# A decode step of attention and a gated feed-forward: another second maximum, another way to turn q, another order of loads and of the first V products

## The chip, the cores and the metric

The kernel runs on one core of one Trainium2 chip. The metric is the device time of one execution in microseconds (us), as the median of several runs. All inputs lie in the chip's HBM at the start, and the output lies there at the end. Beside the timed runs one execution was taken with the hardware profiler; times inside the kernel come from that one.

The engines are named as in the profile: PE (matrix multiply; PEld is its weight load), DVE (vector), ACT (scalar, with the exp table), POOL (GpSimd) and SP (which issues the loads). Each works through its own list of instructions in order, and waits on semaphores for the others.

## The reference

Two batch rows `x` of 448 values are layer-normalised. Branch A is attention of one new token against the last 2048 cached positions (16 query heads, 8 key/value heads, head width 256). Branch B is a small ReLU network. The output is `x + A * silu(B)`.

```python
xn = layernorm(x)                                    # [2, 1, 448] bf16
q  = (xn @ wq).reshape(2, 1, 16, 256)                # wq [448, 4096]
k, v = k_cache[:, :, -2048:, :], v_cache[:, :, -2048:, :]   # 8 heads, each used by 2 query heads
p  = softmax(q . k * 256 ** -0.5)
s  = (p . v).reshape(2, 1, 4096) @ wo                # wo [4096, 448]
g  = silu(relu(xn @ w1) @ w2)                        # w1 [448, 1792], w2 [1792, 448]
out = x + s * g
```

## The kernel before, in words

**Units.** The 16 pairs of batch and key/value head are worked in four units (`NU`) of four heads of one batch row: unit u is head group u // 2 of batch row u % 2. The K and the V of a unit are 4 MB each; a partition holds 64 consecutive positions (`NT`) of one head, 256 values each. Three buffers `ub` take the eight loads in turn (`place`): k0, k1 and v0 first, then each load waits for the work that frees its buffer.

**The order of work** is written out by hand at the end of the function (lines 395 to 457). Each helper appends instructions to the engines' lists, with the operations each depends on; `_Prog.run` turns them into semaphore waits. So the order of the calls is the order on every engine.

- `do_turn(u)` (line 254): four DVE transposes turn K into `kt`, 32x32 blocks of 4-byte pairs. It frees k's buffer and needs the scores of the unit before, which read `kt`.
- `do_q()` (line 263): 28 matmuls over seven slots of `wq` put q into PSUM (`obk`), in four groups of partitions. Then ACT and DVE scale and spread the even and the odd values into `q_n` (128x1024 each), 16 matmuls turn them into `mbk`, and four ACT copies of 32 partitions each put them into `qz`, the weights of the score matmuls for all units.
- `do_S(u)` (line 291): 4 mask and 32 score matmuls into `sbk`.
- `do_chain(u)` (line 305): the softmax. DVE takes each partition's maximum (`rm`), PE turns that into one row, DVE takes the second maximum over the partitions of the same head (`mrow`, one partition, written 128 wide), PE spreads it over the partitions again, DVE copies it to `bias`, ACT takes exp, DVE and PE turn the result, and ACT copies it to `pt`.
- `do_sum(u)`, `do_PV(u)`, `do_o(u)` (lines 330, 335, 345): the sums of exp over each head and their reciprocals, 32 V matmuls into `obk`, the scaling into `o_sb`, and four matmuls and a product that put the unit's result into `at_exp`.
- `do_H()`, `do_F()` (lines 362, 380): branch B, two layers; then `wo` (lines 446 to 454), 128 matmuls into `wbk`, and the last two products.

The product with `wo` and the second layer of branch B run as four matmuls side by side, one for each quarter of the 448 columns, with two weight columns (the two batch rows); results lie on partitions 32 i + b.

**Queues.** SP issues all large loads, in the order of the `load` and `pr.dma` calls: k0, wq, k1, v0, k2 (after the turning of k0), v1 (after the turning of k1), k3 (after the V products of unit 0), v2, w1, v3, w2, and wo in five parts. An issue that waits holds up those behind it. ACT issues the loads of `x` and one of the two stores.

The line of the second maximum, of which the change speaks:

```python
v = pr.op(DVE, lambda e: e.tensor_reduce(
    out=view(mrow, 0, [[8, 16], [1, 8]], n=1), in_=view(mbk, 0, [[0, 16], [1, 8], [8, 16]], n=1),
    axis=AX.X, op=ALU.max, negate=True), [m])
```

It reads the 128 partition maxima sixteen times (the step 0 of the input), so that each of the 128 places gets the maximum of its own head.

Of the kernel before, what the change touches and what calls it, by code (L numbers as in the profile page):

```python
# [5 lines left out]
BF = mybir.dt.bfloat16  # L6
F32 = mybir.dt.float32
# [67 lines left out]
def bass_recurrent_scan__sliding_block_cached__dense_activation_relu__decode_kernel(  # L75
# [22 lines left out]
    NU = 4  # L98
# [9 lines left out]
    with es:  # L108
# [27 lines left out]
        xr = named("xr", [128, SLOTS * 4], BF)  # L136
        q_n = named("q_n", [128, 2048], BF)
        qz = named("qz", [128, NU * 8 * 32], BF)
        fold8 = named("fold8", [128, 8], F32)
        h_n = named("h_n", [128, FC], BF)  # L140
        h_sb = named("h_sb", [128, 28], BF)
        x_c = named("x_c", [128, NCOL], BF)
# [13 lines left out]
        at_exp = named("at_exp", [128, 256], BF)  # L156
        at2 = named("at2", [128, 64], BF)
        wqo = named("wqo", [128, 32 * D], BF)
# [16 lines left out]
        def kv_src(u, cache):  # L175
# [5 lines left out]
        p_xc = pr.op(POOL, lambda e: e.memset(x_c[:, :], 0.0))  # L181
        d_xc = [pr.dma(ACTE, view(x_c, 0, [[1, NCOL]], n=4, p0=b, pstep=32),
                       A_x[b, 0, :].rearrange("(i n) -> i n", i=4), [p_xc]) for b in range(B)]

# [13 lines left out]
        p_one = pr.op(POOL, lambda e: e.memset(one_f[:, :], 1.0), [p_idf])  # L198
        p_qz = pr.op(POOL, lambda e: e.memset(qz[:, :], 0.0))

# [19 lines left out]
        def fold_op(e):  # L220
            with nc.allow_low_precision("zeros and ones"):
                return e.tensor_reduce(out=fold[:, :], in_=view(ident, 0, [[1, 32], [32, 4]]), axis=AX.X, op=ALU.add)
        v_fold = pr.op(DVE, fold_op)
        v_fold8 = pr.op(DVE, lambda e: e.tensor_reduce(
            out=fold8[:, :], in_=view(ident, 0, [[1, 8], [8, 16]]), axis=AX.X, op=ALU.add), [p_id])
# [27 lines left out]

        def do_turn(u):
            src = ub[place[f"k{u}"]]
            s32, k32 = src[:, :].bitcast(F32), kt[:, :].bitcast(F32)
            for g in range(4):
                lo, hi = g * UW // 8, (g + 1) * UW // 8
                st["turn", u, g] = pr.op(DVE, lambda e, lo=lo, hi=hi: e.transpose(k32[:, lo:hi], s32[:, lo:hi]),  # L259
                                         [dma_of[f"k{u}"], st.get(("S", u - 1))])  # L260
            freed[f"k{u}"] = st["turn", u, 3]

        def do_q():
            deps = [d_wq, v_xr, st["obz"]]
            for s in range(SLOTS):
                for i in range(4):
                    lo = s * HC + i * 512
                    o = pr.op(PE, mm(obk[32 * i:32 * i + 4, :], xr[:, 4 * s:4 * s + 4], wqo[:, lo:lo + 512],
                                     s == 0, s == SLOTS - 1, tile_position=(0, 32 * i)), deps)
                    deps = []  # L270
            st["q_mm"] = o
            a_z0 = st["obz"]
            v = pr.op(ACTE, lambda e: e.activation(  # L273
                view(q_n, 0, [[256, 8], [32, 4], [1, 32]]), view(obk, 0, [[64, 8], [0, 4], [2, 32]]),
                ACT.Copy, scale=SCALE), [o, a_z0])
            v2 = pr.op(DVE, lambda e: e.tensor_scalar(  # L276
                out=view(q_n, 128, [[256, 8], [32, 4], [1, 32]]), in0=view(obk, 1, [[64, 8], [0, 4], [2, 32]]),
                scalar1=SCALE, scalar2=None, op0=ALU.mult), [v])
            deps = [v, v2, st["mbk"]]
            for ch in range(2):  # L280
                for wp in range(8):
                    o = pr.op(PE, mm(view(mbk, 32 * wp + ch, [[2, 16]]),
                                     view(q_n, 128 * (8 * ch + wp), [[1, 128]]),
                                     view(ident, 0, [[2, 2], [1, 2], [32, 4]]), True, True), deps)
                    deps = []
            for Q in range(4):
                st["q"] = st["mbk"] = pr.op(ACTE, lambda e, Q=Q: e.activation(  # L287
                    view(qz, 8 * Q, [[256, NU], [32, 8], [1, 8]], n=32, p0=32 * Q),
                    view(mbk, 0, [[8, NU], [32, 8], [1, 8]], n=32, p0=32 * Q), ACT.Copy), [o, p_qz])

        def do_S(u):
            deps = [st["q"], st.get(("exp", u - 1)), v_am] + [st["turn", u, g] for g in range(4)]
            for wp in range(-1, 8):
                for g in range(4):
                    if wp < 0:
                        lhsT, rhs = amask[:, :], view(ident, 0, [[0, 128], [1, 4]])
                    else:
                        lhsT = view(qz, 256 * u + 32 * wp, [[1, 32]])
                        rhs = view(kt, g * UW // 4 + 64 * (wp // 2) + wp % 2, [[256, 16], [2, 32]])
                    o = pr.op(PE, mm(sbk[32 * g:32 * g + 32, :], lhsT, rhs, wp < 0, wp == 7,  # L300
                                     tile_position=(0, 32 * g)), deps)
                    deps = []
            st["S", u] = o

        def do_chain(u):
            v = pr.op(DVE, lambda e: e.tensor_reduce(out=rm[:, :], in_=sbk[:, :], axis=AX.X, op=ALU.max),  # L306
# [3 lines left out]
            v = pr.op(DVE, lambda e: e.tensor_reduce(  # L310
                out=view(mrow, 0, [[8, 16], [1, 8]], n=1), in_=view(mbk, 0, [[0, 16], [1, 8], [8, 16]], n=1),
                axis=AX.X, op=ALU.max, negate=True), [m])
            m = pr.op(PE, mm(mbk_ap(128, 1), mrow[0:1, :], one_f[0:1, :], True, True), [v, p_one])
            v = st["mbk"] = pr.op(DVE, lambda e: e.tensor_copy(bias[:, :], mbk_ap(128, 1)), [m])  # L314
            a = st["exp", u] = pr.op(ACTE, lambda e: e.activation(  # L315
                e_sb[:, :], sbk[:, :], ACT.Exp, bias=bias[:, 0:1], accum_out=ssum[:, 0:1]),
                [v, st.get(("ptd", u - 1)), st.get(("gs", u - 1))])
            t = st["ptd", u] = pr.op(DVE, lambda e: e.transpose(ptd[:, :], e_sb[:, :]), [a, st.get(("sp", u - 1))])  # L318
            deps = [t, st.get(("pt", u - 1))]
# [15 lines left out]
        def do_PV(u):  # L335
            v, p = ub[place[f"v{u}"]], pt[u % 2]
            deps = [dma_of[f"v{u}"], st["pt", u], st.get(("osb", u - 1)), st["q"]]
            for k in range(NT // 2):
                g = k % 4
                o = pr.op(PE, mm(obk[32 * g:32 * g + 16, :], view(p, 16 * k, [[1, 16]]),  # L340
                                 v[:, 512 * k:512 * k + 512], k < 4, k >= 28, tile_position=(0, 32 * g)), deps)
                deps = []
            st["PV", u] = freed[f"v{u}"] = o
# [18 lines left out]
        def do_H():  # L362
# [11 lines left out]
            for j in range(7):  # L374
                o = pr.op(PE, mm(fbk[:, 4 * j:4 * j + 4], view(h_n, j, [[7, 128]], n=4), ident[0:4, 0:4], j == 0), deps)
                deps = []
            st["hT"] = pr.op(DVE, lambda e: e.tensor_copy(
                view(h_sb, 0, [[2, 7], [14, 2], [1, 2]]), view(fbk, 0, [[4, 7], [2, 2], [1, 2]])), [o])

        def do_F():  # L380
            deps = [st["w2"], st["hT"], st["fbz"]]
            for f in range(14):
                for i in range(4):
                    lo = f * D + i * NCOL
                    o = pr.op(PE, mm(fbk[32 * i:32 * i + B, 0:NCOL], h_sb[:, 2 * f:2 * f + 2], w2_sb[:, lo:lo + NCOL],
                                     f == 0, f == 13, tile_position=(0, 32 * i)), deps)
                    deps = []
# [5 lines left out]
                out=g_sb[:, :], in0=fbk[:, 0:NCOL], in1=tmp[:, :], op=ALU.mult), [v_rc])  # L393

        load("k0")
        d_wq = pr.dma(SP, wqo[:, 0:SLOTS * HC], wq_src)
        load("k1")
# [4 lines left out]
        do_turn(0)  # L402
        load("k2")
        do_q()
        do_S(0)
        do_chain(0)
        do_sum(0)
        do_turn(1)
        load("v1")
        do_PV(0)  # L410
        load("k3")
        do_o(0)
        do_S(1)
        do_chain(1)
# [25 lines left out]
        for b in range(2):  # L440
            m_at = pr.op(PE, mm(mbk_ap(256 + 32 * b, 32), at_exp[:, 128 * b:128 * b + 128],
                                fold[:, :], True, True), [st["at", 3], v_fold, st["mbk"]])
            v_at2 = st["mbk"] = pr.op(DVE, lambda e, b=b: e.tensor_copy(
                view(at2, b, [[2, 32]]), mbk_ap(256 + 32 * b, 32)), [m_at])
        do_F()
        deps = [v_at2, st["wbz"]]
        landed = dict(d_wo)
        for j in range(32):
            deps = deps + [landed.get(j)]
            for i in range(4):  # L450
                lo = j * D + i * NCOL
                m_o = pr.op(PE, mm(wbk[32 * i:32 * i + B, 0:NCOL], at2[:, 2 * j:2 * j + 2], wqo[:, lo:lo + NCOL],
                                   j == 0, j == 31, tile_position=(0, 32 * i)), deps)
                deps = []
        v_t = pr.op(DVE, lambda e: e.tensor_tensor(
            out=tmp[:, :], in0=wbk[:, 0:NCOL], in1=g_sb[:, :], op=ALU.mult), [m_o, st["g"]])
        v_o = pr.op(DVE, lambda e: e.tensor_tensor(
            out=out_sb[:, :], in0=tmp[:, :], in1=x_c[:, :], op=ALU.add), [v_t, *d_xc])
        d_o = [pr.dma((SP, ACTE)[b], out[b, 0, :].rearrange("(i n) -> i n", i=4),
                      view(out_sb, 0, [[1, NCOL]], n=4, p0=b, pstep=32), [v_o]) for b in range(B)]  # L460
        pr.op(ACTE, None, d_o)

# [29 lines left out]
```

## Time and profile before

| | us |
|---|---|
| median of 3 runs | 126.58 (125.11 to 126.99) |
| the profiled execution, its own time | 126.08 |
| its span, first to last instruction | 124.6 |
| DVE busy / PE busy / ACT busy | 63.6 / 48.0 / 12.5 |
| transposes of K (`kt`), 16 of 2.28 | 35.5 |
| score matmuls / V matmuls, 128 each | 14.0 / 11.6 |
| second maximum (`mrow`), 4 of 2.28 | 9.1 |
| PE waiting for `wq` | 15.9 |

The kernel moves 44.19 MB, on average 355 GB/s over the span. The span in 40 slices of 3.1 us, each digit the busy share in tenths:

```profile
PE   0100000924814380951300496140019516779561
DVE  2620799130172999145599514549980653110341
ACT  2700000038004000002100000210000021000000
PEclk9999999999995555578555559655556995555897
DMA  5797999989798998989899969989997999700000
```

PEclk is the clock granted to PE in tenths of full speed. The runs of 9 on DVE are the turnings of K, the last 15 us have no loads, and no compute engine is busy throughout.

Times after this are microseconds from the span's start, unless they are durations. The chain of waits is the work that ended last, followed back from the last instruction to what released it; it is read as the list of pieces that set the time.

### The profile page before, as it was taken

To read this page: it belongs to the slowest core of one execution; us is meant where nothing else is said; L and a number is where in the kernel's file an instruction comes from. 1 tells how busy PE (TensorE), PEld (TensorE's weight loads), DVE (VectorE), ACT (ScalarE), POOL (GpSimd) and SP (SyncE) were. 2 spreads that over 40 slices of the span, in tenths; PEclk is the share of its full clock that TensorE was granted. 3 is DMA by queue.
4 is the path that set the end of the run, shared out by engine and by line. 5 is a ranking of instruction groups with operands and counts; after the bars stand their busy time and mean duration, and the time that the engine had idled before them with its cause. 6 is when DMAs were issued, how large, how long until landed. Compare 5 with 4: busy or idle time off the path is not lost.

```text
span 124.6 us, 1421 instructions
## 1 busy us (share of the span) xinstructions
PE 48.0 (39%) x630; PEld 20.5 (16%) x630; DVE 63.6 (51%) x69; ACT 12.5 (10%) x24; POOL 2.3 (2%) x11
## 2 busy tenths in 40 slices
PE   0100000924814380951300496140019516779561
PEld 0000000211112110310200131130003204114150
DVE  2620799130172999145599514549980653110341
ACT  2700000038004000002100000210000021000000
POOL 6000000000000000000000000000000000000000
PEclk9999999999995555578555559655556995555897
DMA  5797999989798998989899969989997999700000
GB/s 169 337 505 337 442 442 463 484 358 505 337 505 373 463 473 368 326 358 494 347 494 410 410 263 426 463 345 510 389 484 329 425 418 421 300 6 0 0 5 1
DMA packets 2474, 44.19 MB, mean 355 GB/s; under 512 B 291, under 2 KB 549, under 8 KB 933
## 3 DMA queue, kind: packets, MB, share of 16 engines
q1 hardware_dynamic: 2440, 44.11, 84.2%
q8 instruction: 4, 0.07, 0.2%
q10 hardware_dynamic: 28, 0.00, 0.0%
q14 instruction: 2, 0.01, 0.0%
HBM read 44.11 MB, written 0.00 MB: 354 GB/s over the span
## 4 chain that ended last, share of the span: by engine, by line
DVE 37%; PE 36%; DMA 16%; ACT 5%; issue 4%; SPq 1%
DVE kt L259 20%; DMA wqo<-in_A_wq_dram 16%; PE sbk L233 13%; PE obk L233 9%; DVE mrow L310 7%; PE fbk L233 5%; PE mbk L233 5%; ACT e_sb L315 3%; DVE ptd L318 2%; DVE o_sb L347 2%; PE pbk L233 2%; PE wbk L233 1%; ACT qz L287 1%; DVE rm L306 1%; DVE h_n L370 1%
## 5 line engine op out<-in xcount | busy, mean ns | idle before, releaser
L259 DVE STREAM_TRANSPOSE kt<-ub 128x2048 f32<-128x2048 f32 x16 | 35.5, 2277 | 6.2 <-DMA ub<-in_A_k_cache_dram 6.2
L233 PE MATMUL sbk<-kt,qz 128*32 128x512 bf16 x128 | 14.0, 611 | 0.0
L233 PE MATMUL obk<-ub,pt 128*16 128x512 bf16 x128 | 11.6, 525 | 2.2 <-DMA ub<-in_A_v_cache_dram 2.2
L306 DVE TENSOR_REDUCE rm<-sbk 128x1 f32<-128x512 f32 x4 | 2.8, 692 | 18.0 <-PE sbk L233 18.0
L310 DVE TENSOR_REDUCE mrow<-mbk 1x128 f32<-1x2048 f32 x4 | 9.1, 2278 | 3.7 <-PE mbk L308 3.7
L233 PE MATMUL sbk<-ident,amask 128*32 128x512 bf16 x16 | 2.5, 608 | 19.8 <-DVE kt L259 18.2
L233 PE MATMUL obk<-wqo,xr 128*4 128x512 bf16 x28 | 3.2, 626 | 15.9 <-DMA wqo<-in_A_wq_dram 15.9
L315 ACT ACTIVATE e_sb<-sbk,bias 128x512 bf16<-128x512 f32 x4 | 2.7, 687 | 61.9 <-DVE bias L314 61.9
L233 PEld LDWEIGHTS sbk<-kt,qz 128*32 128x32 bf16 x128 | 4.7, 140 | 7.6 <-issue 7.6
L233 PE MATMUL fbk<-w_sb,xr 128*4 128x448 bf16 x14 | 5.5, 571 | 0.7 <-DVE h_n L370 0.7
L233 PE MATMUL mbk<-one_f,mrow 1*128 1x1 f32 x8 | 1.7, 281 | 9.5 <-DVE mrow L310 9.5
L233 PE MATMUL pbk<-ptd,ident 128*32 128x128 bf16 x64 | 2.5, 307 | 7.2 <-DVE ptd L318 7.2
L233 PEld LDWEIGHTS obk<-ub,pt 128*16 128x16 bf16 x128 | 3.9, 112 | 8.2 <-issue 4.7
L347 DVE TENSOR_SCALAR o_sb<-obk,rs 128x512 bf16<-128x512 f32 x4 | 2.9, 731 | 3.3 <-PE obk L233 3.3
L318 DVE STREAM_TRANSPOSE ptd<-e_sb 128x512 bf16<-128x512 bf16 x4 | 2.8, 711 | 3.4 <-ACT e_sb L315 3.4
L370 DVE TENSOR_SCALAR h_n<-fbk 4x448 bf16<-4x448 f32 x2 | 1.2, 612 | 5.3 <-PE fbk L233 5.3
L233 PEld LDWEIGHTS sbk<-ident,amask 128*32 128x32 bf16 x16 | 0.4, 101 | 20.1 <-DVE kt L259 18.3
L233 PEld LDWEIGHTS obk<-wqo,xr 128*4 128x4 bf16 x28 | 0.8, 114 | 17.5 <-DMA wqo<-in_A_wq_dram 16.0
L233 PE MATMUL mbk<-fold,o_sb 128*128 128x8 bf16 x16 | 1.1, 172 | 6.6 <-DVE o_sb L347 6.6
L276 DVE TENSOR_SCALAR q_n<-obk 128x1024 bf16<-128x1024 f32 x1 | 1.2, 1225 | 3.9 <-ACT q_n L273 3.9
L333 DVE RECIPROCAL rs<-mbk 128x1 f32<-128x1 f32 x4 | 0.7, 168 | 4.9 <-PE mbk L233 4.9
L233 PEld LDWEIGHTS mbk<-one_f,mrow 1*128 1x128 f32 x8 | 1.4, 213 | 10.2 <-DVE mrow L310 10.2
(63 smaller groups left out, 39.1 us busy)
## 6 DMA issues: line engine op xcount, KB each, us to landing
ub<-in_A_k_cache_dram SPq DMA_DIRECT2D x4, 4096.0 KB, 25.6
ub<-in_A_v_cache_dram SPq DMA_DIRECT2D x4, 4096.0 KB, 17.3
wqo<-in_A_wq_dram SPq DMA_DIRECT2D x1, 3584.0 KB, 20.3
w_sb<-in_B_w_dram SPq DMA_DIRECT2D x2, 1568.0 KB, 20.6
wqo<-in_A_wo_dram SPq DMA_DIRECT2D x2, 1120.0 KB, 27.3
wqo<-in_A_wo_dram SPq DMA_DIRECT2D x1, 896.0 KB, 30.1
wqo<-in_A_wo_dram SPq DMA_DIRECT2D x2, 224.0 KB, 30.2
x_c<-in_A_x_dram ACTq DMA_DIRECT2D x2, 0.9 KB
```

The costliest lines, as they stand in the source:

```text
L233: return lambda e: e.matmul(out_ap, lhsT=lhsT, rhs=rhs, start=start, stop=stop, skip_group_check=True, **kw)
L259: st["turn", u, g] = pr.op(DVE, lambda e, lo=lo, hi=hi: e.transpose(k32[:, lo:hi], s32[:, lo:hi]), [dma_of[f"k{u}"], st.get(("S", u - 1))])
L276: v2 = pr.op(DVE, lambda e: e.tensor_scalar(out=view(q_n, 128, [[256, 8], [32, 4], [1, 32]]), in0=view(obk, 1, [[64, 8], [0, 4], [2, 32]]) ...
L287: st["q"] = st["mbk"] = pr.op(ACTE, lambda e, Q=Q: e.activation(view(qz, 8 * Q, [[256, NU], [32, 8], [1, 8]], n=32, p0=32 * Q), view(mbk, ...
L306: v = pr.op(DVE, lambda e: e.tensor_reduce(out=rm[:, :], in_=sbk[:, :], axis=AX.X, op=ALU.max), [st["S", u]])
L310: v = pr.op(DVE, lambda e: e.tensor_reduce(out=view(mrow, 0, [[8, 16], [1, 8]], n=1), in_=view(mbk, 0, [[0, 16], [1, 8], [8, 16]], n=1), a ...
L315: a = st["exp", u] = pr.op(ACTE, lambda e: e.activation(e_sb[:, :], sbk[:, :], ACT.Exp, bias=bias[:, 0:1], accum_out=ssum[:, 0:1]), [v, st ...
L318: t = st["ptd", u] = pr.op(DVE, lambda e: e.transpose(ptd[:, :], e_sb[:, :]), [a, st.get(("sp", u - 1))])
L333: st["rs", u] = st["mbk"] = pr.op(DVE, lambda e: e.reciprocal(rs[:, u:u + 1], mbk_ap(130, 1)), [st["gs", u]])
L347: st["osb", u] = pr.op(DVE, lambda e: e.tensor_scalar(out=o_sb[:, :], in0=obk[:, :], scalar1=rs[:, u:u + 1], scalar2=None, op0=ALU.mult), ...
L370: st["h_n"] = pr.op(DVE, lambda e, u=u: e.tensor_scalar(out=h_n[0:4, u * (FC // 2):(u + 1) * (FC // 2)], in0=fbk[0:4, 0:FC // 2], scalar1= ...
```

## The change

It does six things.

- The second maximum is taken into a tile `m8` of 1x8, reading the 128 values once, and a copy then spreads it to the 128 places of `mrow`.
- q is turned in another way: one ACT copy of 128x512 out of PSUM, one DVE transpose in 32x32 blocks of 4-byte pairs, four matmuls against `rep4` (made at the start by four DVE products), and eight DVE products with `qmask` that write `qz`, two for each unit. Scores of a unit depend on that unit's two.
- The first slot of `wq` is a load of its own ahead of k0, the other six follow k0, and the q matmuls are split the same way.
- The first quarter of the turning of k1 is placed on DVE between the exp of unit 0 and the transpose of its result.
- The V products and the output step of unit 0 stand behind the scores of unit 1.
- Batch row 1 lies 16 partitions from row 0 in place of 1, in `x_c`, `out_sb` and the results of the last two layers; so `x_c` is loaded, and the output stored, in one DMA each, and the weights `h_sb` and `at2` are 17 columns wide, with zeros between the two.

```diff
-        d_xc = [pr.dma(ACTE, view(x_c, 0, [[1, NCOL]], n=4, p0=b, pstep=32),
-                       A_x[b, 0, :].rearrange("(i n) -> i n", i=4), [p_xc]) for b in range(B)]
+        d_xc = pr.dma(ACTE, view(x_c, 0, [[1, NCOL]], n=8, pstep=16),
+                      A_x[:, 0, :].rearrange("b (i n) -> i b n", i=4), [p_xc])
...
-        p_qz = pr.op(POOL, lambda e: e.memset(qz[:, :], 0.0))
+        p_at = pr.op(POOL, lambda e: e.memset(at2[:, :], 0.0))
+        p_h = pr.op(POOL, lambda e: e.memset(h_sb[:, :], 0.0))
...
+        for i in range(4):
+            v_r4 = pr.op(DVE, lambda e, i=i: e.tensor_scalar(
+                out=view(rep4, 128 * i, [[32, 4], [1, 32]]), in0=view(fold, 0, [[0, 4], [1, 32]]),
+                scalar1=qmask[:, i:i + 1], scalar2=None, op0=ALU.mult), [v_fold, v_qm])
...
+        def do_q():
+            a = pr.op(ACTE, lambda e: e.activation(q_n[:, :], obk[:, :], ACT.Copy, scale=SCALE),
+                      [st["q_mm"], st["obz"]])
+            st["q_n"] = a
+            v = pr.op(DVE, lambda e: e.transpose(q_t[:, :].bitcast(F32), q_n[:, :].bitcast(F32)), [a])
+            deps = [v, v_r4, st["mbk"]]
+            for i in range(4):
+                o = pr.op(PE, mm(mbk_ap(64 * i, 64), rep4[:, 128 * i:128 * i + 128],
+                                 view(q_t, 0, [[64, 8], [1, 8]]), True, True), deps)
+                deps = []
+            for u in range(NU):
+                for par in range(2):
+                    st["qz", u] = st["mbk"] = pr.op(DVE, lambda e, u=u, par=par: e.tensor_tensor(
+                        out=view(qz, 256 * u + 32 * par, [[64, 4], [8, 4], [1, 8]]),
+                        in0=view(mbk, 2 * u + par, [[8, 4], [0, 4], [32, 8]]),
+                        in1=view(qmask, 0, [[0, 4], [1, 4], [0, 8]]), op=ALU.mult), [o, v_qm])
...
             v = pr.op(DVE, lambda e: e.tensor_reduce(
-                out=view(mrow, 0, [[8, 16], [1, 8]], n=1), in_=view(mbk, 0, [[0, 16], [1, 8], [8, 16]], n=1),
-                axis=AX.X, op=ALU.max, negate=True), [m])
+                out=m8[:, :], in_=view(mbk, 0, [[1, 8], [8, 16]], n=1), axis=AX.X, op=ALU.max, negate=True), [m])
+            v = pr.op(DVE, lambda e: e.tensor_copy(
+                view(mrow, 0, [[8, 16], [1, 8]], n=1), view(m8, 0, [[0, 16], [1, 8]], n=1)), [v])
...
+            if between:
+                between()
             t = st["ptd", u] = pr.op(DVE, lambda e: e.transpose(ptd[:, :], e_sb[:, :]), [a, st.get(("sp", u - 1))])
...
-                    o = pr.op(PE, mm(fbk[32 * i:32 * i + B, 0:NCOL], h_sb[:, 2 * f:2 * f + 2], w2_sb[:, lo:lo + NCOL],
+                    o = pr.op(PE, mm(fbk[32 * i:32 * i + 17, 0:NCOL], h_sb[:, 32 * f:32 * f + 17], w2_sb[:, lo:lo + NCOL],
...
+        d_wq = [pr.dma(SP, wqo[:, 0:HC], wq_src[:, 0:HC])]
         load("k0")
-        d_wq = pr.dma(SP, wqo[:, 0:SLOTS * HC], wq_src)
+        d_wq.append(pr.dma(SP, wqo[:, HC:SLOTS * HC], wq_src[:, HC:SLOTS * HC]))
         load("k1")
         load("v0")
...
+        do_q_mm(0, 1)
+        do_q_mm(1, SLOTS)
         do_q()
         do_S(0)
-        do_chain(0)
+        do_chain(0, lambda: do_turn(1, 0, 1))
         do_sum(0)
-        do_turn(1)
+        do_turn(1, 1, 4)
         load("v1")
+        do_S(1)
         do_PV(0)
         load("k3")
         do_o(0)
-        do_S(1)
         do_chain(1)
...
-                m_o = pr.op(PE, mm(wbk[32 * i:32 * i + B, 0:NCOL], at2[:, 2 * j:2 * j + 2], wqo[:, lo:lo + NCOL],
+                m_o = pr.op(PE, mm(wbk[32 * i:32 * i + 17, 0:NCOL], at2[:, 32 * j:32 * j + 17], wqo[:, lo:lo + NCOL],
...
-        d_o = [pr.dma((SP, ACTE)[b], out[b, 0, :].rearrange("(i n) -> i n", i=4),
-                      view(out_sb, 0, [[1, NCOL]], n=4, p0=b, pstep=32), [v_o]) for b in range(B)]
-        pr.op(ACTE, None, d_o)
+        d_o = pr.dma(ACTE, out[:, 0, :].rearrange("b (i n) -> i b n", i=4),
+                     view(out_sb, 0, [[1, NCOL]], n=8, pstep=16), [v_o])
+        pr.op(ACTE, None, [d_o])
```

## The prediction

> **What bounds the kernel now.** I read the page's shares of the chain first, then that chain in order of time, then the timeline around each join, then the loads one by one. The page's chain shares and its line for the load queue:
> ```profile
> q1 hardware_dynamic: 2440, 44.11, 84.2%
> ...
> DVE 37%; PE 36%; DMA 16%; ACT 5%; issue 4%; SPq 1%
> ```
> The load queue is nearly always full until about 110 us, yet the chain goes through a load only once, at the start. After that DVE and PE hand the work to each other, and each saved microsecond on that hand-over counts as long as the loads stay ahead. The chain in order of time (start us, us, what):
> ```profile
> 1.46 20.29 DMA wqo<-in_A_wq_dram
> ...
> 21.78 3.19 PE obk L233 x28
> ...
> 24.99 1.03 ACT q_n L273
> ...
> 26.05 1.24 DVE q_n L276
> ...
> 27.42 0.65 PE mbk L233 x16
> ...
> 29.25 0.39 ACT qz L287
> ...
> 29.68 4.06 PE sbk L233 x36
> ...
> 34.81 2.29 DVE mrow L310
> ```
> From the end of the q matmuls (24.97) to the first scores (29.68) nothing but turning q happens: 4.71 us. Then comes the second maximum, 2.29 us, in every unit. The timeline where unit 0 meets unit 1:
> ```profile
> 40.59 4.49 DVE L259 STREAM_TRANSPOSE kt<-ub 128x2048 f32<-128x2048 f32 x2
> ...
> 42.64 2.74 PE L233 MATMUL obk<-ub,pt 128*16 128x512 bf16 x24 [2.17 <-DMA ub<-in_A_v_cache_dram]
> ...
> 49.39 0.71 DVE L347 TENSOR_SCALAR o_sb<-obk,rs 128x512 bf16<-128x512 f32 x1
> ...
> 50.75 3.63 PE L233 MATMUL sbk<-kt,qz 128*32 128x512 bf16 x32
> ...
> 54.44 0.69 DVE L306 TENSOR_REDUCE rm<-sbk 128x1 f32<-128x512 f32 x1 [3.75 <-PE sbk L233]
> ```
> The V products of unit 0 wait for v0 (42.6), but run beside the turning of k1, which sets the pace until 49.47. The issues of k1 (at 2.06) and v0 (at 2.79), with the time from issue to landing last:
> ```profile
> ub<-in_A_k_cache_dram SPq DMA_DIRECT2D x1, 4096.0 KB, 29.4
> ```
> ```profile
> ub<-in_A_v_cache_dram SPq DMA_DIRECT2D x1, 4096.0 KB, 39.8
> ```
> So k1 lands at 31.5 and v0 at 42.6. From the same view: k0 13.2, wq 21.8, k2 52.4, v1 62.1, k3 71.9, v2 84.0, w1 87.7, v3 97.5, w2 101.2, the last of wo about 110.
>
> **First wq slot, then k0.** The first slot is a seventh of 3.67 MB, 0.52 MB; at the 420 GB/s of those stretches k0 lands 1.3 us later, 14.5, and its turning (8.89 us) ends at 23.4 instead of 22.14. The scores will ask for it at 26.6, so 3.2 us of cover hide it; anything beyond counts in full. wq and k0 together are the same bytes, so wq's rest still lands at 21.8. Slot 0's 4 of 28 matmuls are done long before, and they stand in front of nothing but the other slots. The last 24 take 3.19 - 0.43 = 2.76 (four take 0.427 in the timeline). Ahead of them on DVE, four `rep4` products (0.17 to 0.23 each by L228 and L226) and on POOL two memsets (0.95 by L199, and under half of it) end before 8 us: hidden behind wq. k2's issue slips from 22.17 to 23.4, with k1 and v0 still queued ahead: nothing.
>
> **q turned on DVE.** After the matmuls: ACT copy of 128x512, 0.60 (L327); transpose of 128x256 f32, 0.35 (a 2048-wide one takes 2.277, so 0.28 and a start; upper end 0.71, L318); four matmuls, 0.33 (16 of the old ones took 0.64, four against `fold` 0.27); two products of 128x128, 0.58 (0.275 at 112 wide, L455); hand-overs 0.22. Sum 2.08 against 4.71. Scores of unit 0 start at 21.78 + 2.76 + 2.08 = 26.6, not 29.68: **-3.1** (-2.5 to -3.4). The other six products, 1.7 us of DVE, lie under the 4.06 us of scores, before `rm` needs DVE.
>
> **Second maximum.** A reduce of 128 elements to 8 costs 0.28 to 0.37 (L217, L224) and a 128-wide copy 0.23 (L226); with a hand-over 0.59 against 2.29. All four are on the chain with DVE waiting for nothing else: 4 x 1.70 = **-6.8** (-6.4 to -7.0).
>
> **A quarter of k1's turning during exp.** DVE idles from the end of `bias` to `ptd`, 0.84 us. The quarter (2.28) fills it and pushes `ptd` back, but the quarter has to be done anyway and DVE carries the chain here: **-0.8**. It adds a wait: `ptd`, and with it pt, the sum and the rest of the turning, now stand behind k1. `bias` ends at 37.73 - 3.1 - 1.7 = 32.9 and k1 lands at 31.5: 1.4 us in hand. Turning then ends at 49.47 - 3.1 - 1.7 - 0.8 = 43.9.
>
> **V products behind the scores.** PE now runs S1 and PV0 in one piece from 43.9, v0 long landed. On DVE `osb` and `at` of unit 0 still stand ahead of `rm` of unit 1, so S1's maximum waits for PV0 as well. Before, from the end of turning to `rm`: 54.44 - 49.47 = 4.97. After: S1 and PV0, then `osb` 0.72, four matmuls 0.27, `at` 0.24, hand-overs 0.15. How long S1 and PV0 take hangs on the granted clock; the windows that compare are units 2 and 3, with H before the last PV:
> ```profile
> core 0: us, PE busy (x) PEld busy (x) DVE busy (x) ACT busy (x) POOL busy (x), PEclk, DMA share, GB/s
> ...
> 49.47:54.44 4.97, 4.23 (x40) 1.39 (x40) 0.85 (x3) 0.00 (x0) 0.00 (x0) 0.50 0.87 316
> ...
> 70.14:76.51 6.37, 6.32 (x69) 2.21 (x69) 0.69 (x1) 0.00 (x0) 0.00 (x0) 0.60 0.87 327
> ...
> 92.86:98.18 5.32, 5.27 (x69) 2.15 (x69) 0.69 (x1) 0.00 (x0) 0.00 (x0) 0.73 0.94 397
> ...
> 105.25:112.67 7.42, 6.01 (x26) 1.90 (x29) 1.45 (x3) 0.00 (x0) 0.00 (x0) 0.50 0.42 166
> ```
> The same pair took 6.3 in unit 2 and 5.3 in unit 3; at half clock throughout it is 4.06 + 3.6 = 7.65. I take 6.0: 7.4 against 4.97, **+2.4** (+1.7 to +4.1). The Trainium skill, "TensorE: Matmul & The Clock Gate", Part 1, says that about 3.4 us of sustained work in a free-running window lifts the clock. By it the pair would take an estimated 5.5 to 7.2 us and the kernel 117.4 to 119.1, but the last window above held 0.50 through 7.4 us at 81% busy, so the rule is no promise.
> PV0 ends at 49.9, so k3 is issued as before (50.07); v1, ahead of it on SP, goes from 49.49 to 43.9, v2 and v3 go about 5 us earlier. k3 (by 71.9) is needed at 77, v2 (by 84) at 90, v3 (by 97.5) at 104, wo's first rows (earlier than 110, as the dips of the load rate near 50 and 71 us close) at 111. The loads stay hidden; the closest is wo.
>
> **Seventeen weight columns, one store, one load of x_c.** 184 matmuls in F and W load 17 columns instead of 2. The W loads start 12.3 ns apart (101 in 1.31 us, mean 84 ns); the 32-column loads of `pbk` start 14.7 ns apart (16 in 0.35, mean 129). Between 0 and 184 x 2.4 ns = 0.44: I take **+0.2**. The same page of the Trainium skill, section "LDWEIGHTS (loading the stationary operand)", charges columns/1.2 ns, an estimated 12.5 ns more each, 2.3 us in all and 120.0 in the end if every load stood in line; the `pbk` loads start closer together than that rule's own time for one. The store takes about 2.0 us from `out_sb` to the end either way, 0 (-0.1 to +0.2): the two issues ran side by side (0.66 and 0.56). The 1.14 us in which PE waits inside W for no data stay, as far as I can tell (0 to -1.1). One x_c load fewer saves 0.56 of ACT's issue at 1.3 us, beside nothing.
>
> **Sum.** -3.1 - 6.8 - 0.8 + 2.4 + 0.2 = -8.1. The profiled execution has a span of 124.6 in a time of 126.08, so 1.48 around it: 116.5 + 1.5 = 118.0. The median shown, 126.58, lies 0.5 above that execution, inside the spread of 125.1 to 127.0; I predict **118.0**.
>
> **Rivals.**
> - *PE prices at their upper end*: S1 and PV0 at half clock (+1.7) and the weight loads in line (+0.4, or past it by up to 1): 120 to 121. For it, S1 ran at 0.50 and H held 0.50 throughout; against it, both pairs of this length lifted the clock. 0.14.
> - *PE speeds up early*: with the q step shorter, the q matmuls and S0 follow within 2.1 us and the clock lifts inside S0. It gains up to 1.4, until `bias` meets k1's landing, and with unit 1's pair at 5.3: 115.9. Against it, S0 ran at the slow pace 4.7 us behind the same matmuls. 0.08.
> - *The wait for k1 takes the place of what was saved* (slower). If the engines serve k1 and v0 side by side, k1 lands with v0 at 42.6, the quarter starts 9.7 us after `bias` and all of unit 0 behind it slips by that: 118.0 + 9.7 = 127.7. It decides from a landing at 41.0 (32.9 + 8.1); past 44 the kernel is slower by over 2%. For it, three loads are queued at once and v0's issue stands 0.7 behind k1's. Against it, landings come in order of issue (13.2, 21.8, 31.5, 42.6), 8.6 to 11.1 apart as their bytes at 380 to 430 GB/s would have it. 0.04.
> - *The change doesn't do what it says*: the small reduce stays near 2.3 because one partition out of PSUM is slow whatever its length. Then 118.0 + 6.8 = 124.8. Against it, 2048 elements in 2.278 us are 1.11 ns each, what the transposes take. 0.03.
>
> **How the numbers follow.** The forecast has 0.71, by itself 116.4 to 119.6. Two per cent of 126.58, about what this measurement can tell from no change, is 2.5 us, so faster means under 124.05. Faster: 0.71 + 0.14 + 0.08 = 0.93. Same: the last rival and the half of the k1 case at 127.7, 0.05. Slower: the half of it with a landing past 44, 0.02. The range takes in the two PE cases, 115.7 to 121.
>
> **What would show it.** `mrow`'s reduce below 0.4 us with a copy near 0.23; S0 starting near 26.6; no idle DVE between `bias` and the first quarter; one PE stretch of S1 and PV0 from 44 to 50 with `rm` behind it near 51; F and W no longer than before. I am wrong if `ptd` of unit 0 waits on k1, if a load ends the wait ahead of turning 2 or 3, PV3 or W, or if W grows by over half a microsecond.

## The result, and the profile after

| | before | after |
|---|---|---|
| median of the runs | 126.78 us (4 runs) | 111.9 us (4 runs, 111.12 to 112.37) |
| ratio, with its 95% interval | | 0.886 (0.874 to 0.897) |
| profiled execution, its own time | 126.08 | 111.12 |
| its span | 124.6 | 109.6 |
| PE busy / DVE busy | 48.0 / 63.6 | 41.1 / 58.5 |

The kernel is 11% faster: 14.9 us gained, where 8.1 were forecast, and 111.9 lies below the range of 115.7 to 121. Some runs of a kernel lie more than 1.5% above its fastest one: here and below the ratios leave these out, while the medians take in all runs. The load queue and the chain shares on the page after:

```profile
q1 hardware_dynamic: 2576, 44.11, 94.3%
...
DVE 33%; PE 32%; DMA 26%; issue 4%; ACT 2%; SPq 1%
```

The same 44.11 MB fill the queue 94% of a shorter span, so little is left to gain as long as all of them are loaded. The chain after in order of time (start us, us, what):

```profile
2.43 28.64 DMA ub<-in_A_k_cache_dram
...
31.09 2.31 DVE kt L267
...
42.04 3.71 PE sbk L241 x20
45.75 1.76 PE obk L241 x32
...
49.82 0.29 DVE m L317
...
50.13 0.23 DVE mrow L319
...
92.85 2.53 PE fbk L241 x7
...
96.06 1.66 PE fbk L241 x7
...
98.95 1.86 PE obk L241 x32
...
104.15 2.66 PE wbk L241 x113
```

The second maximum is 0.29 + 0.23. The first quarter of k1's turning waits for the landing of k1 (31.07), not for `bias`. H takes 2.53 and then 1.66 where both halves took 2.7 to 2.8, the V products of unit 3 1.86 where they took 3.55, and the `wo` matmuls are slower than before (113 in 2.66 against 100 in 1.23). The halves of H and the last V products in the chain before:

```profile
105.25 2.71 PE fbk L233 x7
...
108.66 2.79 PE fbk L233 x7
...
112.67 3.55 PE obk L233 x31
```

The scores of unit 0 in the timeline after (start, us, engine, line, operation):

```profile
26.17 0.40 PE L241 MATMUL sbk<-ident,amask 128*32 128x512 bf16 x4 [0.58 <-DVE qz L293]
26.40 2.02 PE L241 MATMUL sbk<-kt,qz 128*32 128x512 bf16 x32
...
28.47 0.69 DVE L313 TENSOR_REDUCE rm<-sbk 128x1 f32<-128x512 f32 x1 [1.17 <-PE sbk L241]
```

They start at 26.17 (forecast 26.6) but take 2.25 instead of 4.06. The stretches of PE after, as windows: the pairs of units 1 (with the output step), 2 and 3, and H:

```profile
core 0: us, PE busy (x) PEld busy (x) DVE busy (x) ACT busy (x) POOL busy (x), PEclk, DMA share, GB/s
42.00:48.86 6.86, 5.69 (x72) 2.26 (x72) 0.98 (x3) 0.00 (x0) 0.00 (x0) 0.77 1.05 454
62.73:68.09 5.36, 5.32 (x69) 2.10 (x69) 0.69 (x1) 0.00 (x0) 0.00 (x0) 0.72 1.10 474
82.07:87.95 5.88, 5.84 (x69) 2.18 (x69) 0.69 (x1) 0.00 (x0) 0.00 (x0) 0.65 1.08 465
92.85:98.95 6.10, 4.69 (x25) 1.66 (x29) 1.45 (x3) 0.00 (x0) 0.00 (x0) 0.72 0.99 418
```

H, at clock 0.50 throughout before, has 0.72. The landings (issue to landing last), k1 and the last parts of `wo`:

```profile
ub<-in_A_k_cache_dram SPq DMA_DIRECT2D x1, 4096.0 KB, 28.6
```
```profile
wqo<-in_A_wo_dram SPq DMA_DIRECT2D x2, 224.0 KB, 35.1
```

The five `wo` issues begin at 69.36 and last 2.4 us, so the last part lands near 106.4; PE uses it from 106.9.

Laid side by side, stage by stage along the chain (us; forecast as the sum had it, each column adding up to its span):

| stage | before | forecast | after |
|---|---|---|---|
| to the scores of unit 0 | 29.68 | 26.6 | 26.17 |
| scores of unit 0 | 4.06 | 4.06 | 2.25 |
| to the end of k1's turning | 15.73 | 13.2 | 13.58 |
| to `rm` of unit 1 | 4.97 | 7.4 | 6.86 |
| to the end of k2's turning | 15.70 | 14.0 | 13.87 |
| scores 2, V products 1 | 6.37 | 6.37 | 5.36 |
| to the end of k3's turning | 16.35 | 14.65 | 13.98 |
| scores 3, V products 2 | 5.32 | 5.32 | 5.88 |
| to H | 7.07 | 5.37 | 4.90 |
| H | 7.42 | 7.42 | 6.10 |
| V products 3 to F | 5.62 | 5.62 | 4.04 |
| F and `wo` | 3.71 | 3.9 | 4.33 |
| to the end | 2.6 | 2.6 | 2.28 |

The missing 6.9 us lie mostly in rows whose own PE work the change leaves as it was: scores of unit 0 (-1.8), unit 2's pair (-1.0), H (-1.3), the last V products (-1.6), with part of the small PE steps of the softmax.

### The profile page after: what moved, and what is told of

Same layout as the page of the kernel before. It is cut to its first block, busy times and chain, and to the rows that moved or that the text cites. A ratio compares the mean times of both kernels' runs of the same rounds, so it can differ in the third digit from the quotient of the medians.

```text
span 109.6 us, 1408 instructions
## 1 busy us (share of the span) xinstructions
PE 41.1 (37%) x618; PEld 19.8 (18%) x618; DVE 58.5 (53%) x85; ACT 10.6 (10%) x20; POOL 2.7 (2%) x12
## 3 DMA queue, kind: packets, MB, share of 16 engines
q1 hardware_dynamic: 2576, 44.11, 94.3%
HBM read 44.11 MB, written 0.00 MB: 402 GB/s over the span
## 4 chain that ended last, share of the span: by engine, by line
DVE 33%; PE 32%; DMA 26%; issue 4%; ACT 2%; SPq 1%
DMA ub<-in_A_k_cache_dram 26%; DVE kt L267 22%; PE sbk L241 10%; PE obk L241 7%; PE fbk L241 5%; PE mbk L241 4%; PE wbk L241 3%; DVE o_sb L357 3%; DVE ptd L328 3%; ACT e_sb L323 2%; PE pbk L241 2%; SPq L36 1%; DVE h_n L380 1%; DVE m L317 1%; PE mbk L315 1%
## 5 line engine op out<-in xcount | busy, mean ns | idle before, releaser
L241 PE MATMUL sbk<-kt,qz 128*32 128x512 bf16 x128 | 12.2, 541 | 0.0
L241 PE MATMUL obk<-ub,pt 128*16 128x512 bf16 x128 | 7.7, 383 | 0.0
L241 PE MATMUL fbk<-w_sb,xr 128*4 128x448 bf16 x14 | 4.2, 458 | 0.7 <-DVE h_n L380 0.7
L241 PEld LDWEIGHTS obk<-ub,pt 128*16 128x16 bf16 x128 | 3.4, 92 | 3.8 <-issue 0.9
L241 PE MATMUL wbk<-wqo,at 128*17 128x112 bf16 x128 | 3.3, 291 | 0.1
L337 ACT ACTIVATE pt<-pbk 128x512 bf16<-128x512 f32 x4 | 2.4, 597 | 7.2 <-PE pbk L241 7.2
L241 PEld LDWEIGHTS wbk<-wqo,at 128*17 128x17 bf16 x128 | 3.0, 136 | 0.3 <-issue 0.3
L241 PEld LDWEIGHTS pbk<-ptd,ident 128*32 128x32 bf16 x64 | 1.2, 112 | 9.3 <-DVE ptd L328 9.3
L317 DVE TENSOR_REDUCE m<-mbk 1x8 f32<-1x128 f32 x4 | 1.1, 278 | 3.2 <-PE mbk L315 3.2
```

Of the source, the lines that this page charges most:

```text
L241: return lambda e: e.matmul(out_ap, lhsT=lhsT, rhs=rhs, start=start, stop=stop, skip_group_check=True, **kw)
L317: v = pr.op(DVE, lambda e: e.tensor_reduce(out=m8[:, :], in_=view(mbk, 0, [[1, 8], [8, 16]], n=1), axis=AX.X, op=ALU.max, negate=True), [m])
L337: st["pt", u] = pr.op(ACTE, lambda e: e.activation(pt[u % 2][:, :], pbk[:, :], ACT.Copy), [o, st.get(("PV", u - 2))])
```

## The experiments

Theory A says that these rows follow PE's granted clock, which switches on a fixed grid of time, so that the placing of PE's work on the grid decides. Theory B says that a shorter chain speeds PE up by itself, or that the changed parts were underpriced. Times are medians, unless single runs are named.

**The maximum alone, and q alone**, each put into the kernel before by itself. The maximum:

```diff
+                out=m8[:, :], in_=view(mbk, 0, [[1, 8], [8, 16]], n=1), axis=AX.X, op=ALU.max, negate=True), [m])
+            v = pr.op(DVE, lambda e: e.tensor_copy(
+                view(mrow, 0, [[8, 16], [1, 8]], n=1), view(m8, 0, [[0, 16], [1, 8]], n=1)), [v])
```

> The kernel before with the second maximum alone changed (1x8, then a copy). Priced by rows: 4 x 1.70 us less, 126.8 - 6.8 = 120.0 us. Theory A (the rest of the gain is PE's granted clock, which lifts on a fixed grid of 3.41 us windows, so that only the placing of PE's work on the grid matters): 120.0, give or take 2 as the stretches fall on the grid, with reduce plus copy near 0.55 us in each unit. Theory B (a shorter chain keeps PE warm by itself, and the maximum was underpriced): 117 or less. If the small reduce costs as much as the large one: 126.8.

119.25 us against 126.5 before, from four runs that lie far apart (116.57, 118.52, 119.98, 120.46). The gain is 6 to 10 us by run, so the 6.8 that were priced are neither confirmed nor refuted to better than that, and the lowest run, of which there is no profile, is where theory B had it (117 or less). In the profile, of the run at 118.52, reduce and copy take 0.278 and 0.215, as priced, and with the short maximum in place the last V products still took 3.38 and H both its slow halves (2.72 and 2.79).

q alone (the new `do_q` of the change, with all 28 matmuls ahead of it):

```diff
+            a = pr.op(ACTE, lambda e: e.activation(q_n[:, :], obk[:, :], ACT.Copy, scale=SCALE),
+                      [st["q_mm"], st["obz"]])
...
+            v = pr.op(DVE, lambda e: e.transpose(q_t[:, :].bitcast(F32), q_n[:, :].bitcast(F32)), [a])
```

> The kernel before with q turned on DVE alone (wq still one load behind k0, 28 matmuls in one piece). Priced by rows: 3.1 - 0.4 (the slot stays) = 2.7 us less, 124.1 us, with the first score matmuls near 26.6 to 27.0 and taking 4.06. Theory A: a further 1.8 only if a window of the grid happens to be four fifths full of q matmuls, so that the scores of unit 0 run at full clock. Theory B: the short gap between q matmuls and scores lifts the clock in any case, 122.3.

122.36 us by the median of runs at 120.5, 120.8, 123.9 and 124.3; the ratio of 0.953 (0.945 to 0.961) goes by the lower two. So 4.1 to 5.9 less, where 2.7 was priced. The median is the 122.3 of theory B, but the profile (of the run at 120.8) meets theory A's condition as well: the q matmuls fill the window from 21.93 to 0.90, and the scores of unit 0, from 27.07 to 29.36, run at full pace. Its chain no longer passes through q: it comes from the landing of v0 (42.7), through V products of 3.44, to the scores of unit 1 at 47.27, against 50.42 before. The end of its chain:

```profile
99.72 2.71 PE fbk L238 x7
...
103.13 2.79 PE fbk L238 x7
...
107.14 3.55 PE obk L238 x23
```

H begins 5.5 us earlier than before, and its halves and the last V products take exactly what they took (2.71, 2.79, 3.55). So a shorter chain by itself is not enough.

**Rows side by side again**, two weight columns, in the changed kernel:

```diff
-                m_o = pr.op(PE, mm(wbk[32 * i:32 * i + 17, 0:NCOL], at2[:, 32 * j:32 * j + 17], wqo[:, lo:lo + NCOL],
+                m_o = pr.op(PE, mm(wbk[32 * i:32 * i + B, 0:NCOL], at2[:, 2 * j:2 * j + 2], wqo[:, lo:lo + NCOL],
```

> The changed kernel with the two batch rows side by side again (2 weight columns in the last two layers, two stores, two x_c loads). By the prediction's price of the 17 columns, 0.2 us less. By the trace after (23.6 ns for each wo matmul against 12.3, 21 against 15 in the second layer), 1.8 less in those matmuls, of which the wait of 1.1 us inside W that is nearly gone after comes back, and 0.3 more at the store: 111.9 - 0.4 = 111.5. If the 17 columns don't matter and the slower pace has another cause: 112.2.

114.23 us (112.74 to 114.84; the lower two 112.74 and 113.61), not faster than with 17 columns. The `wo` line of its chain, and the F line of the timeline of the filled kernel below, whose clock is at 1.00 there:

```profile
107.38 2.69 PE wbk L239 x113
```
```profile
98.82 0.87 PE L242 MATMUL fbk<-w_sb,h_sb 128*17 128x112 bf16 x56
```

Two columns at half clock: 2.69 / 113 = 23.8 ns each, as 17 columns did after (2.66 / 113 = 23.5). Seventeen columns at full clock: 56 in 0.87, as two columns before (0.86). So the columns cost nothing that these rows show; the slower `wo` matmuls after are the clock, 0.50 from 103.2 to 106.6. The expectation, mine by then, that the columns cost 1.8 us was wrong. What this kernel takes more, 0.8 to 2.9 us by run, is not in these matmuls: in its profile, of a run at 114.84, every load from k0 on landed 1.9 us later.

**x_c in two loads again**, to see whether that delays them:

```diff
+        d_xc = [pr.dma(ACTE, view(x_c, 0, [[1, NCOL]], n=4, p0=16 * b, pstep=32),
+                       A_x[b, 0, :].rearrange("(i n) -> i n", i=4), [p_xc]) for b in range(B)]
```

> The changed kernel with x_c loaded in two DMAs again (all else as changed, 17 columns and one store too). In the run with the rows side by side every load from k0 on landed 1.9 us later. If two small loads beside the leading wq slot do that: k0 landing near 16.0, wq near 23.2, and about 1.9 more, 113.8 us. If it was chance or the narrow weights: 111.9.

113.12 us (111.34 to 113.58; its lower two, 111.34 and 112.89, are hardly above the changed kernel's). In the profile, of the run at 113.58, wq landed at 21.8, only 0.45 later than after. Not the 1.9; the cause of that stays open.

**V products first again:**

```diff
-        do_S(1)
         do_PV(0)
         load("k3")
         do_o(0)
+        do_S(1)
         do_chain(1)
```

> The changed kernel with the V products and output step of unit 0 ahead of the scores of unit 1 again. V0 lands near 41.8, when the turning of k1 ends (42.0): the V products take 1.8 to 3.6, the output step 1.2, and then the scores 4.1, so the maximum of unit 1 starts near 50.7 instead of 48.9: 113.7 us if the clock does as it likes at half speed for both, 112 if it lifts for the scores. If the move was a loss, as the prediction had it by about 1 us: 111 or less.

113.35 us by the median (111.22, 113.17, 113.54, 117.94), against 112.05 for the changed kernel run again (below). The chain of the run at 113.54:

```profile
3.03 39.13 DMA ub<-in_A_v_cache_dram
...
42.20 3.62 PE obk L241 x24
...
46.92 3.99 PE sbk L241 x31
...
50.94 0.70 DVE rm L313
```

Once k1 is turned by 42, v0's landing ends the wait, and both stretches run at half clock behind one another. `rm` of unit 1 starts at 50.9 against 48.9 and 49.6 in the two profiles of the changed order. But the lowest run, 111.22, of which there is no profile, is as fast as the changed kernel's. So a gain of the move, 1.3 to 2 us in this profile, is not shown by the times.

**PE kept busy.** Matmuls whose result nobody reads fill PE's waits, so that the clock is up when the real work comes; no other instruction is changed. Once in the kernel before, once in the changed one, with numbers fitted to the waits of each (a part is shown):

```diff
+        dbk = psum("dbk", [128, 512], F32)
+        def fill(n, deps=()):
+            for k in range(n):
+                pr.op(PE, mm(dbk[:, :], ident[:, :], view(ident, 0, [[0, 4], [1, 128]]), True, True), deps if k == 0 else ())
...
+        fill(5)
+        fill(5, [st["turn", 2, 0]])
+        fill(6, [st["turn", 2, 1]])
+        fill(8, [st["turn", 2, 2]])
         do_S(2)
```

> The kernel before with idle PE time filled by matmuls whose result nobody reads (512 columns against the identity, into a PSUM bank of their own), placed so that PE has worked for more than two of the 3.41 us windows when each stretch of scores, H and the last V products begin. Nothing else moves. Theory A (the unforeseen 6 us of the change are the granted clock): scores of unit 0 2.2 instead of 4.06, unit 1 about 2.2 instead of 4.0, unit 2 pair 4.1 instead of 6.3, unit 3 pair 4.1 instead of 5.3, H 5.0 instead of 7.4, the last V products 1.9 instead of 3.6: about 11 less, 116 us, and a smaller spread. Theory B (the clock follows the shorter chain and is worth little by itself): within 2 us of 126.5, or slower by the fill matmuls that stand in the way.

114.56 us (114.5 to 115.36), ratio 0.903 (0.899 to 0.907). Without any part of the change, the kernel before gains 12.5 us of 127 (12.3 by the runs that the ratio takes). Its chain:

```profile
49.08 2.20 PE sbk L234 x33
...
67.27 2.23 PE sbk L234 x33
69.49 1.73 PE obk L234 x31
...
98.01 1.43 PE fbk L234 x7
...
102.86 1.86 PE obk L234 x32
```

Scores in 2.2 instead of 4.0, the half of H in 1.43 instead of 2.71, the last V products in 1.86 instead of 3.55. Only the V products of unit 0, behind the landing of v0, kept half pace (3.59). That is theory A, in size too: 116 was expected. Theory B expected no more than 2 us of this, and falls here as the account of the missing time.

> The changed kernel with the same filling. By PE alone about 6 us less than 111.9 (pairs 4.1 instead of 5.3 to 5.8, H 5.0 instead of 6.1, wo at full clock 1.6 instead of 3.1), 106. But the last part of wo landed at 106.4 in the trace after, 0.5 us before PE reached it, so theory A has the loads as the bound now: last load near 106, end near 109 in the span, 109 to 110.5 us, with PE waiting for wo. Theory B: 111.9.

111.1 us (110.62 to 111.47), ratio 0.874 (0.870 to 0.878). The end of its chain, and PE's waits in `wo`:

```profile
68.01 37.97 DMA wqo<-in_A_wo_dram
106.02 1.47 PE wbk L242 x48
```
```profile
PE wbk L242 <- DMA wqo<-in_A_wo_dram: 4.5, 3, 1.9
```

PE is ready for `wo` at 99.7 and waits 4.5 us for it, in three pieces. Filled, the changed kernel gains 0.9 us and the loads set the time; the expectation held. So the change is worth 3.5 us (114.56 to 111.1) where PE's clock is up in both, with the loads as the floor of the second.

The changed kernel as it is, once more:

> The changed kernel once more, for its spread and for another placing on the clock's grid. Theory A: times from 111 to 114, with stretches of scores and V products between 4.1 and 7.6 us depending on where the switch times, 3.41 us or a multiple apart, fall. Theory B: the same clock pattern every time, 111.1 to 112.4.

112.05 us (111.7 to 115.44). Scores of unit 0 at 3.52 where the first profile had 2.25, with the other stretches as there (5.44, 5.32, 5.84): one stretch changed, the pattern as a whole did not.

```profile
26.24 3.52 PE sbk L241 x27
```

The gap between q's matmuls and these scores is the same in both, so the gap is not what decides. The clock record in a trace begins with the first rise. In the first profile that is at 24.74, behind a window that q's matmuls fill to 0.80; here q's matmuls fall across a switch time, fill two windows to 0.65 and 0.83, and the clock rises at 28.92, amid the scores. Before, it first rose at 34.28, when the scores of unit 0 had ended.

**Filling from the last softmax on only**, in the kernel before:

```diff
+            if u == 3:
+                fill(8)
             m = pr.op(PE, mm(mbk_ap(128, 1), mrow[0:1, :], one_f[0:1, :], True, True), [v, p_one])
...
+                fill(2)
                 st["h_n"] = pr.op(DVE, lambda e, u=u: e.tensor_scalar(
```

> The kernel before with the filling matmuls only from the softmax of unit 3 on. If the clock in H and the last V products is a good part of the unforeseen gain: H 5.0 instead of 7.4, the last V products 1.9 instead of 3.6, the small matmuls of the last softmax 0.4 less, so 4.5 less than 127, 122.5 us, where the fill adds nothing to the chain; against 12.5 for the filling everywhere, so the scores' stretches are worth the other 8. If H and the last V products are slow for another reason: 127 or more.

121.36 us (120.33 to 122.31) against 126.03, 4.7 less by the medians; the ratio, 0.954 (0.947 to 0.961), goes by the lower two runs and makes it 5.9. H and the last V products in its chain:

```profile
105.86 1.43 PE fbk L234 x7
...
110.71 1.86 PE obk L234 x32
```

From the start of H to the last V products 4.85 where it was 7.42, and these in 1.86. From the start of H to the end of the span that profile, of a run at 122.27, has 14.9 us where it was 19.4: the tail is worth about 4.5, and so the scores' stretches most of the other 8 of the 12.5.

**The quarter back, and one wq load.** The quarter:

```diff
-        do_chain(0, lambda: do_turn(1, 0, 1))
+        do_chain(0)
         do_sum(0)
-        do_turn(1, 1, 4)
+        do_turn(1)
```

> The changed kernel with the first quarter of k1's turning back behind the sum of unit 0. By the prediction's price 0.8 more, 112.8 us; DVE idle 0.84 between bias and ptd and the turning of k1 ending 0.8 later. Where the wait for k1 (0.4 in the trace after) takes the place of the idle time, 0.4 more: 112.4.

114.82 us (113.85 to 116.41), where 112.4 to 112.8 was expected. In its profile k1's turning ends at 42.29, 0.3 later than after, since the wait for k1 (0.42) is gone and the scores ended 0.1 earlier; but unit 1's pair then takes 6.81 instead of 5.47. More is lost to the clock behind the quarter than by it.

The load:

```diff
-        d_wq = [pr.dma(SP, wqo[:, 0:HC], wq_src[:, 0:HC])]
         load("k0")
-        d_wq.append(pr.dma(SP, wqo[:, HC:SLOTS * HC], wq_src[:, HC:SLOTS * HC]))
+        d_wq = [pr.dma(SP, wqo[:, 0:SLOTS * HC], wq_src)]
```

> The changed kernel with wq as one load behind k0 again. k0 lands 0.8 earlier (13.3), which nobody needs; wq lands at 21.8 instead of 21.4 and all 28 matmuls follow it: 0.4 + 0.4 later for the scores of unit 0, 112.8 us. The prediction had only the 0.4 of the matmuls.

114.43 us by the median (112.42, 113.88, 114.99, 115.34); 112.8 was expected, and lies between the lower two. In the profile, of the run at 115.34, wq lands at 21.6 and the scores start at 27.0, as expected (0.8 later); what this run takes beyond that is again stretches at half clock (4.06 for unit 0, 6.49 for unit 1's pair).

**Filled up to the end**, the filled changed kernel with more ahead of rows 0, 10 and 20 of `wo`:

```diff
             deps = deps + [landed.get(j)]
+            fill({0: 6, 10: 7, 20: 4}.get(j, 0))
```

> The changed kernel filled as before and also while PE waits for the parts of wo (6, 7 and 4 matmuls ahead of rows 0, 10 and 20), so that the last 48 wo matmuls run at full clock: 0.6 instead of 1.47 behind the last landing near 106. 0.8 less than 111.1: 110.3 us, bound by the loads. If the fill stands in the way of rows that have landed: 111 or more.

110.93 us (110.65 to 111.06, 6 runs), ratio 0.878 (0.875 to 0.882), where 110.3 was expected. The clock is 1.00 through all of `wo`, but the last `wo` landed at 106.6 in this profile. No gain beyond 111.1 that can be told; the loads bind.

**Where the clock switches.** Read in steps of 0.1 us, PEclk after falls or rises at 31.6, 45.2, 52.0, 65.7, 72.5, 86.2, 93.0, 96.4, 103.2 and 106.7. All steps between them are one, two or four times 3.41 us. Laid on that grid, PE's busy share of a window, and what the clock does at its end:

| kernel | window from | filled | clock in it, next |
|---|---|---|---|
| before | 51.35 (scores 1) | 0.89 | 0.5, up |
| before | 41.11 (V products 0) | 0.55 | 0.5, stays |
| before | 105.96, 109.38 (H) | 0.79, 0.79 | 0.5, stays |
| before | 112.79 (V products 3) | 1.00 | 0.5, up |
| maximum alone | 97.30, 100.71 (H) | 0.79, 0.79 | 0.5, stays |
| after | 41.80, 62.28, 82.76 (scores) | 0.93, 0.86, 1.00 | 0.5, up |
| after | 93.00 (H) | 0.79 | 0.5, up |
| after | 89.59 (softmax 3) | 0.33 | 1.0, down |
| changed, run again | 93.77 (H) | 0.79 | 0.5, up |
| V products first | 44.63 | 0.75 | 0.5, stays |

Before, the clock came up at 54.77, when the scores of unit 1 had just ended at 54.41, and at 116.2, when the last V products had. After, H began just before the clock went down at 93.0, filled 0.79 of the next window and had the clock back for its second half and the V products.

**What the placing makes of equal work.** A pair of scores and V products takes 7.65 us at half clock throughout (the prediction's sum). If it runs at half pace until the clock's next rise and at twice that from there, a pair that waits r us for the rise takes (7.65 + r) / 2. Ten pairs of the profiles, by the rise in their own clock records:

| kernel, unit's pair | starts | clock rises | worked out | took |
|---|---|---|---|---|
| after, 1 | 42.04 | 45.22 | 5.4 | 5.47 |
| after again, 1 | 42.85 | 45.99 | 5.4 | 5.44 |
| rows side by side, 1 | 45.19 | 48.82 | 5.6 | 5.66 |
| x_c in two loads, 1 | 43.88 | 48.21 | 6.0 | 6.00 |
| one wq load, 1 | 44.46 | 49.79 | 6.5 | 6.49 |
| quarter back, 1 | 42.33 | 48.29 | 6.8 | 6.81 |
| before, 2 | 70.19 | 75.24 | 6.4 | 6.33 |
| after, 2 | 62.77 | 65.70 | 5.3 | 5.32 |
| before, 3 | 92.91 | 95.72 | 5.2 | 5.28 |
| after, 3 | 82.11 | 86.18 | 5.9 | 5.84 |

All agree within 0.1 us, the gain in unit 2 and the loss in unit 3 with them. So for these stretches the place of the work on the grid accounts for the time.

## Why the prediction was right in its mechanism and wrong in its size

- **First wq slot, then k0.** Turning ended in time, q's matmuls started at 21.39 instead of 21.8, and the short first issue (0.36 against 0.65) would account for most of that; putting wq back cost 0.8 at the scores.
- **q turned on DVE.** From the last q matmul to the scores 2.05 against the priced 2.08. Right.
- **Second maximum.** 0.54 against the priced 0.59 in each unit. Right; the time of the maximum alone is too scattered to tell more.
- **A quarter of k1's turning.** The wait that was named took effect: k1 landed at 31.07 as forecast (31.5), but `bias` came at 30.7, not 32.9, since the scores were fast. DVE, and `ptd` behind it, waited 0.42 us, which the prediction had named as a sign of being wrong.
- **V products behind the scores.** +1.9 against +2.4 on the join as it was. What the step did not weigh is the join that the faster chain would have had in the old order: with k1 turned by 42.0 and v0 landing at 42.2, the V products would have had no turning left to run beside, and in that profile `rm` came 1.3 to 2 us later still. The move is priced against the wrong neighbour, though the sum was little off; what the move itself is worth stays open.
- **Seventeen weight columns.** 0 against +0.2, and against the estimated 2.3 us by the Trainium skill's rule ("TensorE: Matmul & The Clock Gate", section "LDWEIGHTS (loading the stationary operand)"); the row was the better guide, but on the chip even it was too high. One store: 0.3 less than before to the end.
- **The loads stay hidden.** Right, but with 0.5 us to spare at `wo`, and none once PE is fast.
- **The sum, where the prediction failed.** It added the change's parts to the profiled execution and so carried PE's untouched stretches over at the pace they had there: scores of unit 0 at 4.06, unit 2's pair at 6.37, H at 7.42, the last V products at 3.55. Only unit 1's pair got bounds for the clock. Those four were 5.7 us shorter after, while unit 3's pair and the `wo` matmuls were 0.5 each longer at half clock. The rival "PE speeds up early" had the mechanism, with a chance of 0.08, but let it act on unit 0 and unit 1 alone (-2.1), and put it down to the shorter gap behind q's matmuls, which the changed kernel run again does not bear out. The filled kernel shows that half clock cost the kernel before at least 12 us; that was the bound to put into the range.
- **The clock rule.** The Trainium skill's page "TensorE: Matmul & The Clock Gate", Part 1, speaks of a free-running window of about 3.4 us, and the switch times agree. The prediction held H against it ("no promise"); H was the case on the edge, its windows filled to 0.79, not a counterexample.

Theory B fell with q alone, whose shorter chain left H and the last V products as slow as they were, and with the filled kernel before. H, with its windows filled to 0.79, lifted the clock in all seven unfilled kernels that were profiled with both q and the maximum changed, and not in the three with one or neither. The traces show a difference between them: in the seven, the window followed directly on one at full clock, in the three on one at half clock. Why that counts is open. So is how far the 6.9 us beyond the forecast are owed to the change's shorter chain or to where it happened to put PE's work: of eight runs seven gave 111.1 to 112.4 and one 115.4, so the pattern is mostly the same from run to run, but the two profiles have unit 1's scores at nearly the same place on the grid (0.23 and 0.27 us behind a switch time), and whether that is luck they can't tell. Holding PE at half clock in the changed kernel wasn't tried.

## What to carry to other kernels

Before summing edits on a profile, mark which stretches of PE ran at half clock and price each at both paces: a change that moves them by a microsecond can be worth as much as the work it removes. Where PE waits for another engine between bursts of 4 to 8 us, first fill the waits with matmuls that nobody reads, sized to stay clear of the chain; only then is what an edit is worth seen. And look what binds next: here the loads, 44.11 MB, end the gain near 111 us.

## What the runs showed of the hardware

- The clock switches on a grid of 3.41 us, in all fourteen profiles. At half clock, windows that PE filled to 0.92 or more always brought it up, and windows filled to 0.75 or less never did. At 0.82 to 0.91 eleven did and three did not (0.83, 0.84 and 0.91, all in the filled kernel before). At 0.76 to 0.81 the nine that followed directly on a window at full clock did, and the seven that followed on one at half clock did not. From full clock, windows filled to 0.47 or less brought it down, 0.58 or more did not, and 0.48 to 0.57 did both.
- Four matmuls side by side with 112 columns each start 12 ns apart at full clock and 23.5 at half, with 2 or 17 weight columns alike.
- Before the first rise in a trace's clock record PEclk reads 1.00 even where matmuls run at half pace (scores of unit 0 before: 4.06 at "1.00", 4.06 at 0.50 for unit 1). The pace of equal matmuls is the safer reading.
- PE can stop once inside `wo` without waiting for data. Before, this came after 100 of the 128 matmuls and lasted 1.14 us; with 12 PE matmuls fewer it came after 113 in five kernels (in three more no stop shows), with 23 more after 77, and with 111 more after 117. So its place goes by PE's count of instructions, to within one matmul if it comes back every 128. At half clock it was 0.1 to 0.8 us, at full clock 0.9 to 1.9. What PE waits for there was not tested.
